# A fused attention and two mixture layers on one core: where an activation copy, tile clears and a split stand in the queues

## The chip, the cores and the metric

The kernel runs on one core of one Trainium2 chip. The metric is the time of one execution in microseconds on the device; lower is better. The core has five engines, each with its own queue: TensorE (PE) multiplies, VectorE (DVE) and ScalarE (ACT) work element by element, GpSimd (POOL) does so too and issues scatters, SyncE (SP) issues DMAs. An engine takes its instructions in the order of its queue. Where two engines depend on each other, one waits on a semaphore.

## The reference, cut to what matters

```python
q_bits = (np.einsum('bhsd,dk->bhsk', q, proj) > 0)
mask = q_bucket[:, :, :, None] == k_bucket[:, :, None, :]
scores = np.where(mask, scale * np.matmul(q, k.transpose(0, 1, 3, 2)), -1000000000.0)
...
h = x @ w_in
sp = np.where(h > 20.0, h, np.log1p(np.exp(np.minimum(h, 20.0))))
x = (h * np.tanh(sp)) @ w_out
...
expert_idx = np.argmax(logits, axis=1)
h = np.maximum(x[mask] @ w1[e], 0.0)
out[mask] = gate_w[mask, None] * (h @ w2[e])
```

Attention has 2 batches, 8 heads, 768 tokens and 64 dimensions; a query sees only keys with the same six hash bits. Its output, 1536 tokens by 512, goes through a dense layer of 2048 hidden units with the activation h·tanh(softplus(h)), and then through one of eight experts of 1024 hidden units.

## The kernel before

**Numbers as pairs.** To keep precision with 16-bit matmuls, most operands are held as two f16 planes, a rounded upper half and the remainder. A product is then three matmuls (upper by upper, upper by lower, lower by upper). ACT usually writes the upper half, and DVE or POOL subtracts to get the lower one.

**Attention** (`Attn`). The constructor makes the constant tiles. There are three tiles `kq` of 128 x 1572 f16 (`NBUF`), used in turn by the heads; line 167 clears each, line 168 sets one column. Lines 172 to 190 clear parts of the tiles `vn` and `sv`. A first head is loaded; `hi` (L265, ACT) makes the upper halves of k and q, `lo` (L271, DVE) the lower halves, one plane at a time, `dup` (L286) copies the upper planes into the head's `kq` tile, next to where `bits` (L307 to L309, DVE) writes the hash planes. `out_x` turns the halves on PE (L229) into PSUM, and the `cx` steps (L231) copy the result out, plane 0 on ACT, plane 1 on DVE. `proj` (L196 to L201, DVE) splits the hash projection in three, and `args` (L297, PE) multiplies with it. The first steps of heads 0 to 4 are written out by hand in `PRO` (line 51), one line a step; a letter at the end (a, d, s, o, m) names the engine of a copy or the PSUM pool. `run_all` (L488) issues them in that order, and `in_order` (L124) makes every engine keep it. From then on a table of due times (`AT`) places the steps of each head in the loop over groups g. The constants ahead of `run_all` are outside `in_order`: the framework's scheduler places them in the queues.

**Other constants** (`Moe.__init__`, L621 to L651) come earlier in the program: biases, iotas, a tile of ones, and `ohacc`, a small count of 128 x 8. Line 646 clears it on POOL, line 647 writes its first row (eight numbers) on DVE.

**The dense layer** (`moe1`, L809). A step G covers one block of 128 hidden units for a chunk of 512 tokens; there are 3 chunks of 16 blocks, 48 steps, and three more to drain. PE's products are `up` (L790, 12 matmuls, into a PSUM tile h) and x2 (L851, 12 matmuls, adding g of step G - 3 to four sums x2). Up to step 21 (`AHEAD`) the up products run three steps ahead, over four PSUM buffers; in steps 22 to 24 there are none; from step 25 each step makes its own, over two buffers. A buffer of h comes free when L878 has read it.

The activation is a polynomial in tanh. In step G, ACT does L871 (tanh of h), L876 and L882 (squares), L885 (a copy that makes the upper half of g for block G - 1), L888 (Exp), and L900 (a square) for block G. DVE does L873 and L878 for block G - 1, whose result L885 and L886 take, and L895 for block G, which needs Exp's result. POOL does L886, the lower half of g. L895 and L873 read two SBUF tiles each. `fill` (L818) puts side work between them: weight pieces (`w2_load`, L1129 on ACT and L1130 on DVE) and `route`. When a chunk's x2 is complete (f == NF1 - 1, so in steps 18, 34 and 50), `route` (L909) copies its rows out (L923 ACT, L924 DVE), squares them (L930 POOL, L931 ACT), makes logits (L948, PE) and scatters rows to experts (L1036, POOL). The last chunk's route runs alone, with PE's transposes at L936. The whole layer is issued inside `in_order`.

**The experts** (`moe2`, L1148). Per expert 96 up and 48 down matmuls, while the next expert's weights are loaded and split.

Of the kernel before, what the change touches and what calls it, by code (L numbers as in the profile page):

```python
# [15 lines left out]
AF = mybir.ActivationFunctionType  # L16
ALU = mybir.AluOpType
# [25 lines left out]
NBUF, NVB, KXB, KMB = 3, 2, 5, 4  # L43
# [11 lines left out]
lo 0 1  # L55
x 0 s
cx 0 0 a
dup 0 d
proj
cx 0 1 d  # L60
hi 1
warm 0
warm 2
# [71 lines left out]
class Attn:  # L135
    def __init__(self, tc, ctx, q, k, v, proj, ident, ones, xx, dt, rest):
        self.tc, self.nc = tc, tc.nc
        nc = self.nc
        self.q, self.k, self.v = q, k, v
        self.ident, self.ones = ident, ones  # L140
        self.xx, self.rest_pools = xx, rest
        self.ld = ctx.enter_context(tc.tile_pool(name="ld", bufs=2))
        self.st = ctx.enter_context(tc.tile_pool(name="st", bufs=2))
        self.pp = ctx.enter_context(tc.tile_pool(name="pp", bufs=2))
        self.sm = ctx.enter_context(tc.tile_pool(name="sm", bufs=2))
        self.ou = ctx.enter_context(tc.tile_pool(name="ou", bufs=1))
        self.dt = dt
        cp = ctx.enter_context(tc.tile_pool(name="acp", bufs=1))
        self.ps_s = ctx.enter_context(tc.tile_pool(name="ps_s", bufs=2, space=PSUM))
        self.ps_m = ctx.enter_context(tc.tile_pool(name="ps_m", bufs=2, space=PSUM))  # L150
        self.ps_o = ctx.enter_context(tc.tile_pool(name="ps_o", bufs=2, space=PSUM))

        self.Z = {}
        warm = cp.tile([P, 1], F32, name="warm")
        nc.vector.memset(warm, 0.0)
        nc.scalar.activation(warm, warm, AF.Exp)
        pj = cp.tile([P, NB], F32, name="pj")

        def load_pj():
            for i in range(2):  # L160
                nc.sync.dma_start(pj[i * D : (i + 1) * D, :], proj)

        self.load_kq(0, 0, load_pj)
        self.KQ, self.VN, self.SV = [], [], []
        for i in range(NBUF):
            kq = cp.tile([P, 2 * KQW], F16, name=f"kq{i}")
            nc.gpsimd.memset(kq, 0.0)
            nc.gpsimd.memset(self.rows(kq, 780)[:, 0, :, 96:97], 1024.0)
            self.KQ.append(kq)


        for i in range(NVB):
            vn = cp.tile([P, NJ, 65 + P], F32, name=f"vn{i}")
            nc.gpsimd.memset(vn[:, :, 64:66], 1.0)
            nc.gpsimd.memset(vn[:, :, 66 : 65 + 64], 0.0)
            self.VN.append(vn)
        self.sel = cp.tile([P, 3], F32, name="sel")
        nc.gpsimd.memset(self.sel, 64.0)
        nc.gpsimd.memset(self.sel[:, 0:1], 0.0)
        self.c98 = cp.tile([P, 1], F32, name="c98")  # L180
        nc.gpsimd.iota(self.c98, pattern=[[0, 1]], base=0, channel_multiplier=1, allow_small_or_imprecise_dtypes=True)
        c97 = cp.tile([P, 1], F32, name="c97")
        nc.vector.tensor_scalar(c97, self.c98, 97.0, 64.0 * S, op0=ALU.is_equal, op1=ALU.mult)
        nc.vector.tensor_scalar(self.c98, self.c98, 98.0, -1.0, op0=ALU.is_equal, op1=ALU.mult)
        for i in range(2):
            sv = cp.tile([P, 3 * P], F16, name=f"sv{i}")
            nc.gpsimd.memset(sv, 0.0)
            for c in (64, P):
                nc.vector.tensor_copy(sv[96:99, c : c + 1], c97[96:99, :])
            self.SV.append(sv)  # L190

        self.pj = cp.tile([P, 3, NB], F16, name="pj3")
        pr = cp.tile([P, NB], F32, name="pjr")
        C = 1.5 * 2.0**17

        def split():  # L196
            nc.vector.tensor_scalar(self.pj[:, 0], pj, C, C, op0=ALU.add, op1=ALU.subtract)
            nc.vector.tensor_tensor(pr, pj, self.pj[:, 0], op=ALU.subtract)
            nc.vector.tensor_copy(self.pj[:, 1], pr)
            nc.vector.tensor_tensor(pr, pr, self.pj[:, 1], op=ALU.subtract)  # L200
            nc.vector.tensor_copy(self.pj[:, 2], pr)  # L201

        self.proj = split
# [397 lines left out]
CAP = 256  # L601
# [15 lines left out]
C1, C2, C3 = 0.48890862, -0.94632237, -0.89895009  # L617


class Moe:  # L620
    def __init__(self, tc, ctx, a, ident, xh, xl):  # L621
        self.tc, self.nc, self.a, self.ident, self.xh, self.xl = tc, tc.nc, a, ident, xh, xl
        nc = self.nc
        cp = self.cp = ctx.enter_context(tc.tile_pool(name="mcp", bufs=1))
        self.dr = ctx.enter_context(tc.tile_pool(name="dr", bufs=1, space=bass.MemoryType.DRAM))
        self.xs = self.dr.tile([E0 * CAP, ROW], U32, name="xs")
        self.xr = self.dr.tile([NT // P, P, ROW], U32, name="xr")

        self.half = cp.tile([P, NR], F32, name="half")
        nc.gpsimd.memset(self.half, 0.5)  # L630
        self.bias = {}
        for v in (0.5, -1.5, C2, C3):
            t = cp.tile([P, 1], F32, name=f"bias{len(self.bias)}")
            nc.gpsimd.memset(t, v)
            self.bias[v] = t
        self.iota = cp.tile([P, NR, E0], F32, name="iota8")
        nc.gpsimd.iota(self.iota, pattern=[[0, NR], [1, E0]], base=0, channel_multiplier=0, allow_small_or_imprecise_dtypes=True)
        self.ones = cp.tile([P, P], F16, name="ones16")
        nc.gpsimd.memset(self.ones, 1.0)
        self.tri = cp.tile([P, P], F16, name="tri")  # L640
        make_upper_triangular(nc, self.tri, val=1.0, diag=False)
        self.tok = cp.tile([P, NT // P], I32, name="tok")
        for b in range(B):
            nc.gpsimd.iota(self.tok[:, b * NJ : (b + 1) * NJ], pattern=[[P, NJ]], base=b * S, channel_multiplier=1)
        self.ohacc = cp.tile([P, E0], F16, name="ohacc")
        nc.gpsimd.memset(self.ohacc, 0.0)
        nc.vector.tensor_scalar(self.ohacc[0:1, :], self.iota[0:1, 0, :], float(CAP), None, op0=ALU.mult)
        self.scat = []
        self.h = {}
        self.later, self.lows, self.soon = [], [], []  # L650
        self.eo = cp.tile([P, NT // P], F32, name="eo")  # L651
# [157 lines left out]
    def moe1(self, side, more):  # L809

        nc, tm = self.nc, self.tm
# [6 lines left out]
        def fill(k=1):  # L818

            nonlocal now  # L820
            for _ in range(k):
                now += 1
                if self.lows:
                    self.lows.pop(0)()
                    continue
                for x in side:
                    if x[0] <= now:
                        x[0] += next(x[1], 1 << 30)
                        side.append(side.pop(side.index(x)))
                        break  # L830

        for G in range(N + GLAG):
            c, F = divmod(G, NF1)
            if G == 0:
                t, w, u, p = m[0] = self.m0
            elif G < N:
                t, w, u, p = m[G] = [T(tag, G) for tag in "twup"]
# [31 lines left out]
            new_step = 0 < G < N  # L869
# [11 lines left out]
            if new_step:  # L881
                nc.scalar.activation(u, w, AF.Square, scale=C1, bias=self.bias[C2])  # L882
            fill(FILL[1])
            if old:
                nc.scalar.copy(g[G - 1][:, 0, :], p1)  # L885
                nc.gpsimd.tensor_tensor(g[G - 1][:, 1, :], p1, g[G - 1][:, 0, :], op=ALU.subtract)  # L886
            if new_step:
                nc.scalar.activation(u, u, AF.Exp, bias=self.bias[C3])  # L888
            while self.later:
                self.later.pop(0)()  # L890
            for x in new[:NC]:
# [507 lines left out]
```

## Time and profile before

| | us |
|---|---|
| median of 3 runs | 732.04 |
| lowest and highest run | 731.93, 736.9 |
| the profiled execution | 732.01 |
| its span in the trace | 729.9 |

The span is the time from the first to the last thing that the trace records on the core; the profiled execution's own time is 2.1 us longer. Times of rows are counted from the span's start. A row of a timeline says start, length, engine, line, operation, output<-inputs, and in brackets how long the engine idled before and who released it. Equal instructions that follow one another are merged into one row, with their count. A DVE record can contain time in which the instruction was held.

### The profile page before, as it was taken

To read this page: it belongs to the slowest core of one execution; us is meant where nothing else is said; L and a number is where in the kernel's file an instruction comes from. 1 tells how busy PE (TensorE), PEld (TensorE's weight loads), DVE (VectorE), ACT (ScalarE), POOL (GpSimd) and SP (SyncE) were. 2 spreads that over 40 slices of the span, in tenths; PEclk is the share of its full clock that TensorE was granted. 3 is DMA by queue.
4 is the path that set the end of the run, shared out by engine and by line. 5 is a ranking of instruction groups with operands and counts; after the bars stand their busy time and mean duration, and the time that the engine had idled before them with its cause. 6 is when DMAs were issued, how large, how long until landed. Compare 5 with 4: busy or idle time off the path is not lost. (4 is left out here: it accounts for less than half of the span.)

```text
span 729.9 us, 10738 instructions
## 1 busy us (share of the span) xinstructions
PE 703.9 (96%) x3997; PEld 383.8 (53%) x3997; DVE 463.2 (63%) x778; ACT 478.4 (66%) x735; POOL 191.0 (26%) x213
## 2 busy tenths in 40 slices
PE   7899999999999999999999899999999999999995
PEld 4454445455455544444444444444448666667772
DVE  7877888787777795565566555545556545565540
ACT  4657576676666597888888866877763455464631
POOL 5211323131312352121224334352422101100111
PEclk9999999999999999999999999999998999999999
DMA  6368688999987243310103001120145879799740
GB/s 174 105 184 216 162 215 226 239 220 274 209 208 171 78 146 106 80 59 0 58 29 74 16 1 59 61 52 4 52 152 180 219 222 275 221 227 269 224 143 20
DMA packets 125644, 102.71 MB, mean 141 GB/s; under 512 B 86391, under 2 KB 104823, under 8 KB 125586
## 3 DMA queue, kind: packets, MB, share of 16 engines
q1 hardware_dynamic: 112514, 81.23, 42.4%
q10 hardware_dynamic: 10832, 14.43, 5.6%
q0 software_dynamic: 2240, 6.31, 2.6%
q8 instruction: 33, 0.54, 0.3%
q14 instruction: 25, 0.20, 0.1%
HBM read 63.52 MB, written 24.26 MB: 120 GB/s over the span
## 5 line engine op out<-in xcount | busy, mean ns | idle before, releaser
L414 PE MATMUL o<-p,vn 128*65 128x384 f32 (+1 forms) x384 | 153.9, 487 | 2.5 <-ACT su L439 2.5
L790 PE MATMUL h<-xx,wi 128*128 128x512 f16 x576 | 133.2, 382 | 3.7 <-DVE p L878 3.6
L851 PE MATMUL x<-wo,g 128*128 128x512 f16 x576 | 131.7, 379 | 1.2 <-POOL g L886 0.6
L375 ACT ACTIVATE p<-s 128x768 f32<-128x768 f32 x96 | 77.2, 807 | 47.4 <-PE s L373 42.2
L895 DVE SCALAR_TENSOR_TENSOR p<-w,u 128x512 f32<-128x512 f32 x47 | 52.0, 1106 | 79.2 <-ACT u L888 79.2
L886 POOL TENSOR_TENSOR g<-p,g 128x512 f16<-128x512 f32 x47 | 54.5, 1159 | 158.8 <-ACT g L885 139.6
L790 PEld LDWEIGHTS <-wi 128*128 128x128 f16 x576 | 56.4, 98 | 72.6 <-issue 7.1
L851 PEld LDWEIGHTS <-g 128*128 128x128 f16 x576 | 56.2, 98 | 70.2 <-POOL g L886 1.1
L1188 PE MATMUL y<-b,hh 128*128 128x512 f16 x384 | 84.2, 379 | 0.0
L1174 PEld LDWEIGHTS <-a 128*128 128x128 f16 x768 | 75.1, 98 | 10.8 <-issue 0.6
L337 DVE TENSOR_REDUCE mx<-ms 128x1 f32<-128x512 f32 x96 | 65.4, 688 | 21.9 <-PE ms L336 21.0
L414 PEld LDWEIGHTS o<-p,vn 128*65 128x65 f32 (+1 forms) x384 | 59.0, 163 | 30.7 <-issue 11.6
L1174 PE MATMUL h<-xt,a 128*128 128x256 f16 x672 | 74.7, 273 | 0.3 <-DVE hh L1181 0.3
L900 ACT ACTIVATE t<-p,bias 128x512 f32<-128x512 f32 x47 | 34.0, 722 | 43.6 <-DVE p L895 43.6
L667 DVE SCALAR_TENSOR_TENSOR b<-st,b 128x1024 f16<-128x1024 f32 x28 | 33.1, 1222 | 45.3 <-ACT b L666 45.3
L1188 PEld LDWEIGHTS <-hh 128*128 128x128 f16 x384 | 37.5, 98 | 43.6
L1193 POOL DMA_INDIRECT out_dram<-o,row x16 | 20.7, 1291 | 147.2 <-ACT o L1192 109.1
L666 ACT ACTIVATE b<-st 128x1024 f16<-128x1024 f32 x28 | 28.0, 1048 | 40.9 <-DMA st<-in_moe_w_dram 37.5
L341 DVE TENSOR_REDUCE mx<-ms 128x2 f32<-128x512 f32 x48 | 33.0, 688 | 28.2 <-PE ms L340 28.2
L873 DVE SCALAR_TENSOR_TENSOR t<-t,u 128x512 f32<-128x512 f32 x48 | 33.6, 700 | 24.6 <-ACT t L900 23.8
L371 PE MATMUL s<-tx 128*128 128x384 f16 x192 | 48.2, 333 | 0.0
L729 POOL TENSOR_TENSOR wi<-cv,wi 128x512 f16<-128x512 f32 x16 | 19.7, 1232 | 106.9 <-ACT cv L728 84.0
(197 smaller groups left out, 1031.5 us busy)
## 6 DMA issues: line engine op xcount, KB each, us to landing
st<-in_moe_w_dram SPq DMA_DIRECT2D x32, 1024.0 KB
stg<-in_moe_w_in_dram SPq DMA_DIRECT2D x16, 512.0 KB
stg<-in_moe_w_out_dram SPq DMA_DIRECT2D x16, 512.0 KB
dx<-ka ACTq DMA_DIRECT2D x12, 384.0 KB
dm<-kq ACTq DMA_DIRECT2D x12, 384.0 KB
xs<-zrow SPq DMA_DIRECT2D x16, 257.0 KB
vn<-in_v_dram SPq DMA_DIRECT2D x16, 192.0 KB
rb<-rd SPq DMA_DIRECT2D x16, 192.0 KB
```

The costliest lines, as they stand in the source:

```text
L337: nc.vector.tensor_reduce(z["mx"][:, j, 0:1], s, axis=AX.X, op=ALU.max)
L371: nc.tensor.matmul(s[:, c, :], kq[:, 0, ts], kq[:, 1, c * HS : (c + 1) * HS], start=True, stop=False)
L375: nc.scalar.activation(p.rearrange("p (c n) -> p c n", c=2), s, AF.Exp, scale=2.0**-11)
L414: nc.tensor.matmul(o, self.vn(b, h, t), z["p"][t][:, cs], start=(t == 0), stop=False)
L790: self.nc.tensor.matmul(h, self.wi[wu][:, k, fs], x[:, k, xs], start=(i == 0), stop=(i == 3 * NKT - 1))
L851: nc.tensor.matmul(x2[r], gf[:, gu, rs], self.wo[wu][:, f, :], start=(f == 0 and gu + wu == 0), stop=(f == NF1 - 1 and gu == 1))
L873: nc.vector.scalar_tensor_tensor(t1, t1, 0.75, u1, op0=ALU.add, op1=ALU.mult)
L886: nc.gpsimd.tensor_tensor(g[G - 1][:, 1, :], p1, g[G - 1][:, 0, :], op=ALU.subtract)
L895: nc.vector.scalar_tensor_tensor(p, w, 1.0, u, op0=ALU.add, op1=ALU.mult)
L900: nc.scalar.activation(t, p, AF.Square, bias=self.bias[-1.5])
L1174: nc.tensor.matmul(h[:, v, :], W[0][wu][:, k, fs], xt[e][:, xu * NKT + k, :], start=(i == 0), stop=(i == 3 * NKT - 1))
L1188: nc.tensor.matmul(y[s], hs[F // 2][:, hu, F % 2, s * P : (s + 1) * P], W[1][wu][:, F, :], start=(F == 0 and hu + wu == 0), stop=(F == NF2 ...
```

## The change

- In `PRO`, the step `dup 0 d` (the copy of head 0's upper planes on DVE, L286) moves from before `proj` and the second `cx` to behind them.
- The clears of `kq` at line 167 are put on DVE for the first two tiles; the third stays on POOL. Line 168 stays on POOL for all.
- The small product at line 647 is put on POOL instead of DVE.
- In `moe1`, Exp (L888) is issued ahead of the copy L885 and of L886. DVE's queue keeps its order, and so does POOL's.

```diff
@@ -55,9 +55,9 @@
 x 0 s
 cx 0 0 a
-dup 0 d
 proj
 cx 0 1 d
+dup 0 d
 hi 1
@@ -164,7 +164,7 @@
             kq = cp.tile([P, 2 * KQW], F16, name=f"kq{i}")
-            nc.gpsimd.memset(kq, 0.0)
+            (nc.gpsimd if i == NBUF - 1 else nc.vector).memset(kq, 0.0)
             nc.gpsimd.memset(self.rows(kq, 780)[:, 0, :, 96:97], 1024.0)
@@ -644,7 +644,7 @@
         nc.gpsimd.memset(self.ohacc, 0.0)
-        nc.vector.tensor_scalar(self.ohacc[0:1, :], self.iota[0:1, 0, :], float(CAP), None, op0=ALU.mult)
+        nc.gpsimd.tensor_scalar(self.ohacc[0:1, :], self.iota[0:1, 0, :], float(CAP), None, op0=ALU.mult)
@@ -881,11 +881,11 @@
             fill(FILL[1])
+            if new_step:
+                nc.scalar.activation(u, u, AF.Exp, bias=self.bias[C3])
             if old:
                 nc.scalar.copy(g[G - 1][:, 0, :], p1)
                 nc.gpsimd.tensor_tensor(g[G - 1][:, 1, :], p1, g[G - 1][:, 0, :], op=ALU.subtract)
-            if new_step:
-                nc.scalar.activation(u, u, AF.Exp, bias=self.bias[C3])
             while self.later:
```

## Rows read from the trace of the kernel before

**Rows 1.** The page, busy time: us (share of the span) xinstructions.
```profile
PE 703.9 (96%) x3997; PEld 383.8 (53%) x3997; DVE 463.2 (63%) x778; ACT 478.4 (66%) x735; POOL 191.0 (26%) x213
```

**Rows 2.** What PE waited for: us in total, times, longest us.
```profile
PE h L790 <- DVE p L878: 3.6, 2, 3.2
...
PE psx L229 <- DVE ka L271: 0.8, 1, 0.8
...
PE x L851 <- POOL g L886: 0.6, 1, 0.6
```

**Rows 3.** Timeline of PE about the longest wait.
```profile
411.64 2.75 PE L851 MATMUL x<-wo,g 128*128 128x512 f16 x12
414.23 1.35 PE L948 MATMUL lg<-enT,xt 128*128 128x8 f16 x48
418.82 4.44 PE L790 MATMUL h<-xx,wi 128*128 128x512 f16 x12 [3.24 <-DVE p L878]
```

**Rows 4.** One microsecond behind it: busy times, PEclk, DMA share, GB/s.
```profile
421.00:422.00 1.00, 1.00 (x4) 0.44 (x3) 0.66 (x1) 0.30 (x1) 1.00 (x2) 0.50 0.00 0
```

**Rows 5.** Timeline of ACT, one step of the dense layer.
```profile
302.03 0.72 ACT L900 ACTIVATE t<-p,bias 128x512 f32<-128x512 f32 x1 [1.19 <-DVE p L895]
...
303.27 0.72 ACT L876 ACTIVATE w<-t,bias 128x512 f32<-128x512 f32 x1
304.02 0.72 ACT L882 ACTIVATE u<-w,bias 128x512 f32<-128x512 f32 x1
304.65 0.60 ACT L885 CAST g<-p 128x512 f16<-128x512 f32 x1
305.16 0.72 ACT L888 ACTIVATE u<-u,bias 128x512 f32<-128x512 f32 x1
...
307.07 0.72 ACT L900 ACTIVATE t<-p,bias 128x512 f32<-128x512 f32 x1 [0.68 <-DVE p L895]
```

**Rows 6.** Timeline of DVE, the same step.
```profile
305.98 1.06 DVE L895 SCALAR_TENSOR_TENSOR p<-w,u 128x512 f32<-128x512 f32 x1 [1.78 <-ACT u L888]
```

**Rows 7.** Timeline of POOL, the same step.
```profile
305.33 1.16 POOL L886 TENSOR_TENSOR g<-p,g 128x512 f16<-128x512 f32 x1 [3.88 <-ACT g L885]
```

**Rows 8.** Groups by line, DVE from 284 to 288 us: busy us, mean ns.
```profile
L805 DVE SCALAR_TENSOR_TENSOR w<-w,u 128x512 f32<-128x512 f32 x1 | 0.7, 693 | 4.0 <-ACT u L803 4.0
```

**Rows 9.** Timeline of ACT, in steps 19 and 21.
```profile
382.98 0.62 ACT L885 CAST g<-p 128x512 f16<-128x512 f32 x1 [0.50 <-DVE p L878]
...
395.10 0.61 ACT L931 ACTIVATE sq<-sq 128x512 f32<-128x512 f32 x1
```

**Rows 10.** Timeline of PE, the second chunk's end and the layer's end.
```profile
465.49 2.75 PE L851 MATMUL x<-wo,g 128*128 128x512 f16 x12 [0.26 <-DVE row L924]
468.61 2.75 PE L790 MATMUL h<-xx,wi 128*128 128x512 f16 x12 [0.36 <-DVE p L878]
...
529.73 7.93 PE L851 MATMUL x<-wo,g 128*128 128x512 f16 x36
...
541.37 1.50 PE L936 MATMUL tp<-ident,row 128*128 128x128 f16 x24
```

**Rows 11.** Timeline of DVE, the prologue.
```profile
2.43 4.41 DVE L647 TENSOR_SCALAR ohacc<-iota 1x8 f16<-1x8 f32 x1 [1.55 <-POOL ohacc L646]
4.69 2.15 DVE L271 SCALAR_TENSOR_TENSOR ka<-kq,ka 128x384 f16<-128x384 f32 x2
...
9.87 1.02 DVE L271 SCALAR_TENSOR_TENSOR ka<-kq,ka 128x384 f16<-128x384 f32 x2
10.80 0.35 DVE L286 COPY kq<-ka 128x768 f16<-128x768 f16 x1
```

**Rows 12.** Timeline of POOL, the prologue.
```profile
2.33 4.09 POOL L167 MEMSET kq<- 128x1572 f16 x3
```

**Rows 13.** Timeline of PE, the prologue.
```profile
2.09 4.02 PE L210 MATMUL warmed<-ones 128*128 128x384 f16 x12 [2.09 <-POOL ones L639]
...
6.92 0.84 PE L229 MATMUL psx<-ident,ka 128*128 128x128 f16 x12 [0.82 <-DVE ka L271]
```

## The prediction, written before the kernel was changed

> **What bounds the kernel now.** The page first: TensorE (PE) is busy for 703.9 of 729.9 us [rows 1]. So the end moves only by what PE loses, and the list of what PE waited for comes next [rows 2]. For this change three of its entries count: 3.6 us, in two waits, for VectorE's (DVE) product at L878, which frees a buffer of h; 0.8 us in the prologue for the lower halves of L271; 0.6 us for the activations' lower half from GpSimd (POOL), L886. The chain that ended last shows only the output's scatter.
>
> Then PE's timeline at the longest wait [rows 3]. PE is through with the logits at 414.23 + 1.35 = 415.58, but the next up product starts at 418.82, held for 3.24 us by L878. That product then takes 4.44 us where the x2 product of equally many matmuls took 2.75: the granted clock is 0.50 behind the wait [rows 4], the lower of the two levels, after an engine that stood idle. The one place costs 3.24 + 1.69 = 4.93 us.
>
> Why is L878 late? One step of the dense layer with little side work, on ScalarE (ACT), [rows 5] shows a recurrence: L900 of a step starts at 302.03, L900 of the next at 307.07, a period of 5.04 us. In it ACT copies the activations (L885, 304.65) and only then runs Exp (L888, 305.16). Exp feeds L895 on DVE, which starts at 305.98 and takes 1.06 us [rows 6], and L900 waits for L895. L885 also releases POOL's L886 at 305.33 for 1.16 us [rows 7], so POOL runs just ahead of L895 and across it. The same operation with POOL idle, L805, took 693 ns [rows 8]. PE's two products per step start 414.23 - 411.64 = 2.59 us apart [rows 3], some 5.2 us a step: the recurrence has nothing to spare, and any side work puts it behind PE.
>
> **Exp ahead of the copy.** No instruction is added or removed, 47 steps are reordered. The new period from rows 5, 6 and 8: L900 to L876 1.24, L876 to L882 0.75, L882 to Exp 0.75 (Exp now depends on the instruction just ahead of it, as L882 does on L876), Exp to L895 0.82, L895 0.69, L895's end to L900 0.03. Sum 4.28 us, 0.76 below 5.04: the copy's slot goes (0.51 saved, less 0.12 for the dependence) and L895 is shorter by 0.37, since L886 can start only behind the copy, as L895 ends. Bounds for L895's saving: 0 if POOL still meets it, 0.37 if never; I take 0.37, since Exp to copy's end is 0.63 + 0.60 and Exp to L895's end 0.82 + 0.69, so POOL can overlap a tail at most.
>
> Does that cure the wait? By the code the first chunk's x2 is complete in step 18, where the row copies tie ACT to PE, and the held product (step 27) needs L878 of step 26, some seven steps later. Needed: 3.24 us. Available: 7 x 0.76 = 5.3. Against it, side work shared a gap with nothing before and now shares it with the copy: between Exp and L900, 0.82 + 0.69 + 0.03 - 0.63 = 0.91, less 0.51 for the copy, leaves 0.40. A square like that of L931 (0.61) [rows 9] or a weight copy of the same size overflows by 0.1 to 0.4 with its read-out, about 2.3 us over six steps. For it: in step 19 the copy waited 0.50 us for L878 with Exp behind it [rows 9]; Exp no longer stands there. 5.3 - 2.3 + 0.5 = 3.5 us, which is enough, though barely, and a lead gathered in steps 1 to 17 lets the row copies start at the first finished quarter rather than the last. I take the wait and its slow clock as gone: 4.9 us. What is late next is PE itself: up products then follow at PE's own rate.
>
> Two further places in the dense layer. At the second chunk's end the up products start at 465.49 + 3.12 = 468.61, 0.5 us over 2.59, and x2 at 465.49 was itself held by L924 for 0.26 [rows 10]; with the chain earlier by the copy's slot I take 0.8 for both (bounds 0 and 0.8). At the end, 36 matmuls start at 529.73, so the last dozen could run from 529.73 + 3 x 2.59 = 537.50 to 540.09; the transposes behind it started at 541.37, 1.28 later [rows 10], because copy and L886 of the last step were late. That step has no Exp of its own, but its input comes a slot and a contention earlier, over 1 us: I take 1.2 (0.3 to 1.6). Copies come later by 0.63 within a step; what hides that is the lag of three steps between g and its x2, about 15 us, and four buffers of g. If that cover were gone each step would cost 0.6.
>
> The new order turns the port question round: L886 now runs where L873, which also reads two SBUF tiles, comes up after L900. The Trainium skill (SBUF — State Buffer, Who interferes with whom) says that a DVE instruction with two SBUF inputs and a GpSimd instruction that reads SBUF exclude each other, the first holding on to its end. Rows 6 and 7 agree: L895 ended 0.55 us behind L886. By that rule L873 waits up to 0.3 us per step; it is off the recurrence, so the sum stays, and the rule taken to its extreme is the rival below that ends slower.
>
> **Clears, the small product and the split, in the prologue.** DVE starts L647 at 2.43 and is held for 4.41 us for eight elements, to 6.84; POOL's three clears of kq fill 2.33 to 6.42 [rows 11, 12]. Behind L647 stand L271 and the split (L286), and PE's first transposes start at 6.92, having waited 0.82 [rows 13]. After: POOL does L647 itself and one clear of three; two clears, 2.7 us, leave it. DVE does them from about 0.9 on, with nothing to wait for. Their price on DVE is in no row: from below, the f16 copy of 768 elements at 0.35, so 0.7 each; from above, L271 (384 elements, half of 1.02 for two), so 2.1 each [rows 11]; nearest is POOL's own clear of the same tile at 1.4 [rows 12]. I take 1.4: ready at 3.7, before the first L271 starts at 4.69, so hidden by the wait for the input. At 2.1 each they end at 5.1 and delay L271 by 0.4. The Trainium skill (VectorE: DVE Perf Modes, Zero memsets can be issued as uint32) prices a clear at one cycle per element; with that page's clock an estimate is 1.64 us each, ready at 4.2, and by it the sum would be the same.
>
> L271's two then run 4.69 to 5.7. PE's warm-up product ends at 2.09 + 4.02 = 6.11 [rows 13], which is late next: the transposes gain 6.92 - 6.11 = 0.8 us; with the dear clears DVE is done at 6.1 and the gain is the same less 0.1. L647 on POOL: at least nothing, at most a whole clear's 1.4; POOL still is 1.3 us earlier, and nobody on the path waits for it. Moving L286 behind the second copy adds 0.35 us [rows 11] where DVE waits for the projection's matmuls on PE, and takes it from ahead of the split of proj; cover gone, it costs 0.35. No DMA is issued by any moved step. I take 0.8; bounds -0.7 (an initialising DVE instruction queued ahead of L271 waits for POOL) and 1.3 (a filler of DVE drops out of the path too). DVE and PE carry this shift into the attention loop, whose waits are between engines, not on DMA.
>
> Sum: 4.9 + 0.8 + 1.2 + 0.8 = 7.7, plus some 0.5 of short delays like those above that the list of waits leaves out, 8.2 us. The profiled execution took 732.01 us (span 729.9), the median of the runs is 732.04, so both give 723.8.
>
> **Rivals.** (1) Half a cure: POOL still meets L895, a step gains 0.39. 7 x 0.39 - 2.3 + 0.5 = 0.9, so 2.3 us of the wait stay, and the slow clock with it: 0.9 + 0.8 + 0.6 + 0.4 = 2.7, 729.3. For it: POOL has other work (squares). Against: the order of Exp and copy decides, POOL can't pass the copy. (2) The swap gives nothing, since ACT is the limit and not the recurrence: 0.8 from the prologue, 731.2. Against: ACT stood idle 1.19 us ahead of L900 where a step had no side work [rows 5]. (3) Slower: L873 is held by L886 and, if POOL keeps the port from one instruction to the next, by its square too; L878 comes later, and DVE reaches the next L895 late. It decides from about 1.5 us of holding per step, where the 0.76 is eaten (L873's slack to the next L895 is some 0.8). In seven steps 0.5 each lengthens the wait by 3 us: 732.0 + 3 - 0.8 = 734. Against: L895 took the port as soon as L886 ended. (4) Better: the route behind the dense layer escapes part of its slow clock by the shift: 722.
>
> **Chances.** Forecast 0.67 (own range 722.5 to 726), (1) 0.15, (2) 0.07, (3) 0.05, (4) 0.06. The range, 721 to 729.3, leaves out most of (2) and (3). A measurement of this kernel tells about 1% (7.3 us, 724.7) from no change: faster 0.6 (two thirds or more of the forecast's own case, and the fourth), same 0.35, slower 0.05.
>
> **What would show it.** Right: L895 near 0.7 us; period 4.3 in steps where h is ready; no PE wait for L878 near 407 to 415 and no clock of 0.50 there; first transposes near 6.1; L647 a fraction of a microsecond on POOL. Wrong: L895 still above 1 us, L873 above 1.5 us, the wait at the 27th up product still over 2 us, or clears on DVE that end behind 5 us.

## The result, and the profile after

The changed kernel takes 724.64 us (median of 4 runs, 721.95 to 725.62), the kernel before 733.52 in the same session (4 runs, 731.93 to 736.9). The ratio is 0.9867, 95% interval 0.9827 to 0.9907. The forecast was 723.8, with 721 to 729.3 as its range. The profiled execution took 725.26 us, its span is 723.2; before it was 732.01 and 729.9, so the two traces compared below stand 6.7 us apart, somewhat less than the medians.

The page's busy times, the answer to [rows 1]: PE has lost 4.6 us of busy time for the same matmuls, so part of the gain is products that run faster, and its share rose by a point.

```profile
PE 699.3 (97%) x3997; PEld 382.3 (53%) x3997; DVE 457.2 (63%) x779; ACT 482.8 (67%) x735; POOL 188.5 (26%) x212
```

What PE waited for, as in [rows 2]: the waits for L878, for L271 and for POOL's lower half at L851 have left the list. Third now stands one in the experts, L1174 for L1181, which has grown by 1.8 us.

```profile
PE o L414 <- ACT su L439: 2.5, 3, 0.9
PE warmed L210 <- POOL ones L639: 2.1, 1, 2.1
PE h L1174 <- DVE hh L1181: 2.1, 2, 1.7
```

The same entry before the change:

```profile
PE h L1174 <- DVE hh L1181: 0.3, 1, 0.3
```

PE's timeline at the place of [rows 3], and at the layer's end [rows 10]. The up product of step 27 follows the logits with no bracket, in 2.75 us instead of 4.44. At the end 48 matmuls run in one row and the transposes start 532.44 - 522.08 = 10.36 us behind its first, which is 4 x 2.59: nothing is lost there.

```profile
410.00 2.75 PE L851 MATMUL x<-wo,g 128*128 128x512 f16 x12
412.59 1.35 PE L948 MATMUL lg<-enT,xt 128*128 128x8 f16 x48
413.80 2.75 PE L790 MATMUL h<-xx,wi 128*128 128x512 f16 x12
...
522.08 10.52 PE L851 MATMUL x<-wo,g 128*128 128x512 f16 x48
532.44 1.50 PE L936 MATMUL tp<-ident,row 128*128 128x128 f16 x24
```

The microsecond of [rows 4] again: the clock is 1.00, the upper level.

```profile
421.00:422.00 1.00, 1.00 (x7) 0.47 (x5) 0.94 (x2) 0.00 (x0) 0.26 (x1) 1.00 0.00 0
```

One step on ACT (Exp is now L885, the copy L887), as in [rows 5]: Exp directly behind the square, the copy in the gap while L895 runs, 381.32 - 377.03 = 4.29 us from one L900 to the next, where it was 5.04.

```profile
377.03 0.71 ACT L900 ACTIVATE t<-p,bias 128x512 f32<-128x512 f32 x1
...
379.01 0.72 ACT L882 ACTIVATE u<-w,bias 128x512 f32<-128x512 f32 x1
379.77 0.72 ACT L885 ACTIVATE u<-u,bias 128x512 f32<-128x512 f32 x1
380.39 0.60 ACT L887 CAST g<-p 128x512 f16<-128x512 f32 x1
381.32 0.72 ACT L900 ACTIVATE t<-p,bias 128x512 f32<-128x512 f32 x1 [0.32 <-DVE p L895]
```

DVE and POOL about the same step and the next (POOL's lower half is now L888). L895 takes 0.69 us, against 1.06 in [rows 6], and POOL starts as it ends. The price is paid by L873, L1130 and POOL: at 387.07 L873 takes 1.64 us, held by POOL's square L930, which had itself waited for DVE's L1130, as the order of their ends shows.

```profile
380.59 0.69 DVE L895 SCALAR_TENSOR_TENSOR p<-w,u 128x512 f32<-128x512 f32 x1 [0.81 <-ACT u L885]
382.07 0.77 DVE L873 SCALAR_TENSOR_TENSOR t<-t,u 128x512 f32<-128x512 f32 x1 [0.79 <-ACT t L900]
...
385.86 1.28 DVE L1130 SCALAR_TENSOR_TENSOR b<-st,b 128x512 f16<-128x512 f32 x1 [0.28 <-ACT b L1129]
387.07 1.64 DVE L873 SCALAR_TENSOR_TENSOR t<-t,u 128x512 f32<-128x512 f32 x1
```

POOL's timeline, the same stretch:

```profile
381.07 1.22 POOL L888 TENSOR_TENSOR g<-p,g 128x512 f16<-128x512 f32 x1 [12.82 <-ACT g L887]
...
385.37 1.22 POOL L888 TENSOR_TENSOR g<-p,g 128x512 f16<-128x512 f32 x1 [1.51 <-ACT g L887]
386.56 1.60 POOL L930 TENSOR_TENSOR sq<-row 128x512 f32<-128x512 f16 x1
```

The prologue, to be laid beside [rows 11 to 13]: on DVE the two clears end at 2.56, and nothing holds the first L271 but its input; on POOL one clear is left, and L647 takes 0.53 us; on PE the first transposes start at 5.45, with no wait, behind the warm-up product. DVE's timeline:

```profile
1.02 1.54 DVE L167 MEMSET kq<- 128x786 uint32 x2
4.77 1.03 DVE L271 SCALAR_TENSOR_TENSOR ka<-kq,ka 128x384 f16<-128x384 f32 x2 [2.21 <-ACT ka L265]
...
7.80 0.35 DVE L286 COPY kq<-ka 128x768 f16<-128x768 f16 x1
```

The timeline of POOL there:

```profile
2.33 1.41 POOL L167 MEMSET kq<- 128x1572 f16 x1
...
4.91 0.53 POOL L647 TENSOR_SCALAR ohacc<-iota 1x8 f16<-1x8 f32 x1
```

The timeline of PE there:

```profile
2.09 3.52 PE L210 MATMUL warmed<-ones 128*128 128x384 f16 x12 [2.09 <-POOL ones L639]
5.45 0.92 PE L229 MATMUL psx<-ident,ka 128*128 128x128 f16 x12
```

**Where the time went, by marks on PE.** The marks are the first x2 of the dense layer (L851), the transposes behind its last (L936), and the span's end.

| | first x2 | dense layer: first x2 to transposes | transposes to the end | span |
|---|---|---|---|---|
| before | 297.23 | 244.14 | 188.53 | 729.9 |
| after | 296.04 | 236.40 | 190.76 | 723.2 |

So 1.19 us come from ahead of the dense layer and 7.74 from it, and 2.23 went again in route and experts, 1.8 of which is the longer wait at L1174. Whether that loss belongs to the change is a question for the experiments.

### The profile page after: what moved, and what is told of

It is laid out like the page before. It is cut to its first block, busy times and chain, and to the rows that moved or that the text cites. A ratio compares the mean times of both kernels' runs of the same rounds, so it can differ in the third digit from the quotient of the medians.

```text
span 723.2 us, 10738 instructions
## 1 busy us (share of the span) xinstructions
PE 699.3 (97%) x3997; PEld 382.3 (53%) x3997; DVE 457.2 (63%) x779; ACT 482.8 (67%) x735; POOL 188.5 (26%) x212
## 5 line engine op out<-in xcount | busy, mean ns | idle before, releaser
L790 PE MATMUL h<-xx,wi 128*128 128x512 f16 x576 | 131.5, 379 | 0.0
L851 PE MATMUL x<-wo,g 128*128 128x512 f16 x576 | 131.3, 379 | 0.0
L888 POOL TENSOR_TENSOR g<-p,g 128x512 f16<-128x512 f32 x47 | 56.5, 1202 | 152.5 <-ACT g L887 133.8
L851 PEld LDWEIGHTS <-g 128*128 128x128 f16 x576 | 56.4, 98 | 68.0 <-POOL g L888 0.3
L1174 PEld LDWEIGHTS <-a 128*128 128x128 f16 x768 | 75.0, 98 | 12.8 <-issue 2.6
L337 DVE TENSOR_REDUCE mx<-ms 128x1 f32<-128x512 f32 x96 | 65.4, 688 | 21.8 <-PE ms L336 20.8
L1174 PE MATMUL h<-xt,a 128*128 128x256 f16 x672 | 74.8, 273 | 2.1 <-DVE hh L1181 2.1
L895 DVE SCALAR_TENSOR_TENSOR p<-w,u 128x512 f32<-128x512 f32 x47 | 32.5, 692 | 63.2 <-ACT u L885 58.8
L873 DVE SCALAR_TENSOR_TENSOR t<-t,u 128x512 f32<-128x512 f32 x48 | 38.6, 805 | 23.1 <-ACT t L900 22.3
L373 PE MATMUL s<-tm 97*128 97x384 f16 x192 | 47.0, 325 | 0.0
```

The costliest lines, as they stand in the source:

```text
L337: nc.vector.tensor_reduce(z["mx"][:, j, 0:1], s, axis=AX.X, op=ALU.max)
L373: nc.tensor.matmul(s[:, c, :], m[0:97, 0, ts], m[0:97, 1, c * HS : (c + 1) * HS], start=False, stop=True)
L790: self.nc.tensor.matmul(h, self.wi[wu][:, k, fs], x[:, k, xs], start=(i == 0), stop=(i == 3 * NKT - 1))
L851: nc.tensor.matmul(x2[r], gf[:, gu, rs], self.wo[wu][:, f, :], start=(f == 0 and gu + wu == 0), stop=(f == NF1 - 1 and gu == 1))
L873: nc.vector.scalar_tensor_tensor(t1, t1, 0.75, u1, op0=ALU.add, op1=ALU.mult)
L1174: nc.tensor.matmul(h[:, v, :], W[0][wu][:, k, fs], xt[e][:, xu * NKT + k, :], start=(i == 0), stop=(i == 3 * NKT - 1))
```

## The experiments

**The swap alone, and all but the swap.** First the kernel before with Exp ahead of the copy and nothing else.

```diff
+            if new_step:
+                nc.scalar.activation(u, u, AF.Exp, bias=self.bias[C3])
             if old:
                 nc.scalar.copy(g[G - 1][:, 0, :], p1)
...
-            if new_step:
-                nc.scalar.activation(u, u, AF.Exp, bias=self.bias[C3])
```

> Kernel before with Exp ahead of the copy, nothing else. If the dense layer's part is independent of the prologue: first transposes at 6.9 us as before, dense layer (first x2 product to the last route's transposes) near 236.4 us as in the changed kernel instead of 244.1, no wait of PE for L878 behind the logits, L895 near 0.69 us. Time 732 - 7.7 = about 724.5 to 726. Rival (the prologue's shift is needed for it, since it changes where the phases fall): the wait at the up product of step 27 is partly there and the time is above 728.

Measured: 723.75 us (median of 4, 722.83 to 725.83), ratio 0.9853 (0.982 to 0.9887) against 733.13 for before (13 runs). The dense layer took 236.39 us, L895 692 ns in the mean, and the up product of step 27 came without a wait. Then the reverse, the changed kernel with the old order of copy and Exp.

```diff
             if old:
                 nc.scalar.copy(g[G - 1][:, 0, :], p1)
                 nc.gpsimd.tensor_tensor(g[G - 1][:, 1, :], p1, g[G - 1][:, 0, :], op=ALU.subtract)
+            if new_step:
+                nc.scalar.activation(u, u, AF.Exp, bias=self.bias[C3])
```

> Changed kernel with the old order of copy and Exp: only clears, small product and split are moved. Theory: first transposes at 5.4 to 6.1 us, first maximum (L337) at 11.2 to 12.5 instead of 13.6, the dense layer starts 1.2 us earlier and takes the 244 us of before with the wait of about 3.2 us for L878 back. Time 730.5 to 731.3. Rival (the prologue's gain is swallowed in the attention loop): 732, dense layer starting at 297.2.

Measured: 732.35 us (10 runs), ratio 0.999 (0.9968 to 1.0013). The first x2 comes 1.21 us earlier than before, as the theory had it, but the time is the rival's: the dense layer takes 245.28, with the wait back. PE's timeline of this kernel:

```profile
412.74 1.35 PE L948 MATMUL lg<-enT,xt 128*128 128x8 f16 x48
417.63 5.28 PE L790 MATMUL h<-xx,wi 128*128 128x512 f16 x12 [3.54 <-DVE p L878]
```

What follows: the swap makes the whole gain of the dense layer, and all of the gain that a measurement can tell. The layer took 236.39 or 236.40 us in each of the eight profiles here with the swap alone or under other edits of the prologue, and 243.79 to 245.37 in the four that keep the old order and POOL's lower half. The three prologue edits win about a microsecond at the first x2, here and in the first profile of the changed kernel, and none that ten runs can show.

**The changed kernel once more**, to see what spreads by itself; no edit.

> The changed kernel once more, for the spread: the expert phase (from the first expert's up product to the end) took 175.0 us before and 177.1 after in one execution each. If that difference belongs to the change (weights come later relative to PE), it is about 177 here too and PE waits some 2 us for L1181. If it is the spread of the weight loads, it lies between 175 and 178 with other waits. All before that phase should repeat within 0.3 us. Time 722 to 726.

Measured: 723.91 us (4 runs, 721.65 to 727.18), ratio 0.9849 (0.9812 to 0.9887). In this profile the dense layer takes 236.39 again, and PE's waits for L1181 are 0.4 us in all. But the first x2 comes at 300.52, 4.5 us later than in the first profile of the same program, where a repeat within 0.3 was expected. All of it is lost by 95 us: the mean granted clock is 0.94 in the stretches 0 to 30 and 60 to 90 us, 1.00 in the first profile, and PE waits 1.61 us for L307 at 81 us. A third time, in another session:

> The changed kernel a third time, beside the version with both edits of the prologue and the kernel before: 722 to 726 us, dense layer 236.4 us, first x2 between 295.7 and 300.5 us.

Measured: 725.06 us (8 runs, 723.22 to 731.04), ratio 0.9898 (0.9866 to 0.993), dense layer 236.39, first x2 at 295.62. Over the three sessions the median of 16 runs is 724.7 us. In the fourteen profiles of this study the stretch from the transposes to the end took 188.1 to 192.5 us in the nine whose dense layer was cured, and 188.5 to 190.6 in the five others. The wait at L1174 is 0.2 to 3.2 us where it appears. So the 2.23 us lost behind the layer lie within what one program shows from run to run; they are not the change's.

**Only the small product on POOL** (the kernel before, with L647 alone moved).

```diff
-        nc.vector.tensor_scalar(self.ohacc[0:1, :], ...
+        nc.gpsimd.tensor_scalar(self.ohacc[0:1, :], ...
```

> Kernel before with only the small product (L647) on POOL; all three clears of kq stay on POOL, the split stays ahead. Theory (DVE's queue stood behind L647, which POOL's clears held off; L271 itself is not held by clears, which only write): L271 starts near 4.7 and each takes 0.55, first transposes at 5.5 to 6.1 us; the split (L286, a two-port copy) is then the one that is held until a clear ends, near 6.4. Rival (the clears hold every DVE instruction): L271 ends near 6.8 and the transposes start at 6.9 as before.

Measured: 735.98 us (one run). The timeline of DVE in this kernel:

```profile
4.73 1.03 DVE L271 SCALAR_TENSOR_TENSOR ka<-kq,ka 128x384 f16<-128x384 f32 x2 [3.85 <-ACT ka L265]
5.67 1.37 DVE L286 COPY kq<-ka 128x768 f16<-128x768 f16 x1
...
8.40 0.34 DVE L183 TENSOR_SCALAR c<-c 128x1 f32<-128x1 f32 x1
```

and PE's:

```profile
5.66 0.83 PE L229 MATMUL psx<-ident,ka 128*128 128x128 f16 x12
...
8.80 0.47 PE L297 MATMUL ar<-pj,tx 128*128 128x18 f16 x12 [1.98 <-DVE c L183]
```

L271, two SBUF inputs, runs unheld while POOL clears, and the transposes start 1.26 us earlier. But the copy L286 is held to 7.04, past the end of the three clears at 6.42, and a constant of DVE (L183), which the scheduler now puts ahead of the copy that PE needs, waits for a POOL iota behind those clears: PE waits 1.98 us and the hash planes come at 10.06, 0.3 later than before. The edit alone gains nothing.

**Only the clears on DVE** (the kernel before, with line 167 changed).

```diff
-            nc.gpsimd.memset(kq, 0.0)
+            (nc.gpsimd if i == NBUF - 1 else nc.vector).memset(kq, 0.0)
```

> Kernel before with only the two clears on DVE; the small product stays on DVE, the split stays ahead. Theory: L647 is held by POOL's single clear to about 3.8 us, which ends ahead of the first L271 at 4.7: transposes at 5.5 to 6.1 us, as with all three edits. Rival (the small product has to go): L271 later than 5.2 us.

Measured: 732.57 us (one run). L647 is still on DVE and still held, to 4.55 where 3.8 was expected (two small clears of POOL, L175, follow the one of `kq` and end at 4.54), but it ends in time (timeline of DVE in this kernel):

```profile
2.47 2.08 DVE L647 TENSOR_SCALAR ohacc<-iota 1x8 f16<-1x8 f32 x1
4.64 1.03 DVE L271 SCALAR_TENSOR_TENSOR ka<-kq,ka 128x384 f16<-128x384 f32 x2
```

The first hash maximum (L337) starts at 11.04, against 13.60 before and 11.17 after the whole change: the clears alone give the gain at this mark. At the first x2, 297.24, nothing of it is left in this profile. **The split put back ahead of proj** in the changed kernel is the third part:

```diff
 cx 0 0 a
+dup 0 d
 proj
 cx 0 1 d
-dup 0 d
```

> Changed kernel with the split put back ahead of proj and the second copy. Theory: the split takes 0.35 to 0.8 us at 5.7, all of DVE behind it slips by 0.35 to 0.5, so L309 ends 0.3 to 0.5 us later than the 9.0 of the changed kernel; the dense layer starts up to 0.4 us later. Rival (the wait for the projection hides it): L309 at the same time within 0.1.

Measured: 723.75 us (one run). L309 and the first maximum come 0.23 us later (9.05, 11.40) than in the first profile of the changed kernel; in its other two the maximum is at 11.11 and 11.27. Nothing of it is left at the first x2 (295.74). What follows: of the three edits one carries the first maximum, one is worth 0.1 to 0.3 us there, and one only does no harm once the clears are gone.

**Only the contention taken away** (the kernel before, its order kept, the lower half on DVE).

```diff
-                nc.gpsimd.tensor_tensor(g[G - 1][:, 1, :], p1, ...
+                nc.vector.tensor_tensor(g[G - 1][:, 1, :], p1, ...
```

> Kernel before, order of copy and Exp kept, but the lower half of g (L886) is made on DVE instead of POOL: the port question is taken away and the copy's slot stays. Theory (both parts count, 0.39 for the slot and 0.37 for the port): L895 near 0.69 us, period of a quiet step near 4.65 to 4.7, and the wait of PE for L878 behind the logits about 3.2 - 7 x 0.37 = 0.7 us or less. Rival (only the order counts): period stays near 5.04 and the wait near 3.2 us. DVE has 0.7 us more to do per step, which can bring a wait of its own at the chunks' ends.

Measured: 725.7 us (one run), L895 692 ns, and a step of 4.61 us, even with a weight copy in it, which fits the gap behind Exp (timeline of ACT in this kernel):

```profile
356.93 0.72 ACT L900 ACTIVATE t<-p,bias 128x512 f32<-128x512 f32 x1 [0.76 <-DVE p L895]
...
360.69 0.61 ACT L1129 ACTIVATE b<-st 128x512 f16<-128x512 f32 x1
361.54 0.72 ACT L900 ACTIVATE t<-p,bias 128x512 f32<-128x512 f32 x1 [0.24 <-DVE p L895]
```

and PE's timeline at the place of the long wait:

```profile
413.44 1.35 PE L948 MATMUL lg<-enT,xt 128*128 128x8 f16 x48
414.65 2.75 PE L790 MATMUL h<-xx,wi 128*128 128x512 f16 x12
```

The long wait is gone here too, and the dense layer takes 236.89 us, 0.5 more than with the swap. Half of the cure is enough.

**The copy twice** (the changed kernel, L887 issued a second time as L888, to put the price of one copy back without the contention).

```diff
                 nc.scalar.copy(g[G - 1][:, 0, :], p1)
+                nc.scalar.copy(g[G - 1][:, 0, :], p1)
```

> The changed kernel with the copy of the upper half (L887) issued twice in every step of the dense layer that has one: one more ACT instruction of about 0.61 us per step, behind Exp, with the same result. Theory (the recurrence from one L900 to the next sets the pace, and the copy now fills the gap that ACT has while L895 runs): of the gap of about 0.9 us the first copy takes 0.5, so the second overflows by some 0.1 to 0.3 beyond what is left in a quiet step, the period goes from 4.3 to about 4.8 to 4.9, still under PE's 5.2; in steps with side work ACT falls behind by up to 0.6 each. The slack of 1.95 us before the up product of step 27 loses about 7 x 0.5 = 3.5, so a wait for L878 comes back there of some 1.5 us, with the slow clock behind it: dense layer 237.5 to 240 us. Rival (what ACT gathers as a lead in steps 1 to 17, and the time that its row copies wait for PE, covers it, as taking only the contention away did): no wait, dense layer 236.4 to 236.9 us. L895 stays at 0.69 us in both.

Measured: 731.12 us (one run, beside 733.68 of before). A step with nothing else (L901 at 378.04 to L901 at 382.59) takes 4.55 us, less than the 4.8 to 4.9 expected and less than in the experiment above, but a step with a weight copy or a square has no gap left to put it in; the one shown, from ACT's timeline in this kernel, takes 5.14 us:

```profile
409.51 0.71 ACT L901 ACTIVATE t<-p,bias 128x512 f32<-128x512 f32 x1
...
412.87 0.60 ACT L887 CAST g<-p 128x512 f16<-128x512 f32 x1
413.50 0.62 ACT L888 CAST g<-p 128x512 f16<-128x512 f32 x1
414.03 0.62 ACT L932 ACTIVATE sq<-sq 128x512 f32<-128x512 f32 x1
...
414.65 0.71 ACT L901 ACTIVATE t<-p,bias 128x512 f32<-128x512 f32 x1
```

PE's timeline of this kernel, with the wait:

```profile
413.47 1.35 PE L949 MATMUL lg<-enT,xt 128*128 128x8 f16 x48
416.86 2.75 PE L790 MATMUL h<-xx,wi 128*128 128x512 f16 x12 [2.03 <-DVE p L878]
```

The wait returned with 2.03 us where some 1.5 were expected, and the dense layer took 241.76 us, above the 237.5 to 240 of the theory; the rival (a lead that covers all) fell. The layer lost more than the one wait: PE also waited 0.95 for a tile of the route behind it (L996), and 0.25 and 0.68 for g at its end. The slow clock that was expected behind the wait did not come: the product took 2.75.

The four kernels side by side settle how the wait is decided. All times in this table count from the start of PE's x2 row of 36 matmuls (before at 395.96, after at 394.46, lower half on DVE at 395.31, copy twice at 395.34). The first column is L900 behind the first chunk's row copies, the second the same instruction seven steps on, the third the end of the L878 that frees the buffer. PE wants that buffer at 413.80 - 394.46 = 19.34. (The waits in PE's rows, 3.24 and 2.03, are 0.1 to 0.2 shorter than the last column has them.)

| | L900 behind the row copies | L900 seven steps on | L878 ends | against 19.34 |
|---|---|---|---|---|
| before | -16.21 | 20.64 | 22.81 | 3.47 late |
| after | -17.43 | 15.06 | 17.39 | 1.95 early |
| lower half on DVE | -17.43 | 15.69 | 17.86 | 1.48 early |
| copy twice | -17.30 | 19.31 | 21.47 | 2.13 late |

A seventh of the way from the first column to the second is a step: 5.26 us before, 4.64 after, 4.73 and 5.23 in the experiments. What counts over these seven steps is the step with side work, not the quiet one.

The rows behind the first line of the table, from the timelines of ACT and DVE before:

```profile
379.75 0.73 ACT L900 ACTIVATE t<-p,bias 128x512 f32<-128x512 f32 x1
...
416.60 0.72 ACT L900 ACTIVATE t<-p,bias 128x512 f32<-128x512 f32 x1 [0.63 <-DVE p L895]
418.08 0.69 DVE L878 SCALAR_TENSOR_TENSOR p<-t,h 128x512 f32<-128x512 f32 x1
```

and behind the second, after (its first row, L900 at 377.03, is shown above), with one of the copies that came late:

```profile
399.40 0.62 ACT L887 CAST g<-p 128x512 f16<-128x512 f32 x1 [0.34 <-DVE p L878]
...
409.52 0.71 ACT L900 ACTIVATE t<-p,bias 128x512 f32<-128x512 f32 x1
411.16 0.69 DVE L878 SCALAR_TENSOR_TENSOR p<-t,h 128x512 f32<-128x512 f32 x1
```

**What bounds the prologue now.** Two experiments on the changed kernel. In the first the six small constant instructions of lines 183 to 189 go behind the copies of the second product:

```diff
 cm 0 1 d
+consts
...
+        def consts():
```

> Changed kernel with six small constant instructions of DVE (L183, L184, L189) moved behind the copies of the m planes. In the changed kernel they stand between the parts of the split of proj, and PE waits 0.8 us for its last part (L201). Theory: L201 ends near 6.8 instead of 7.4 and the first maximum comes 0.5 us earlier, but the next stage waits for the load of heads 2 and 3 (ACT waited 0.33 us for it), so at most 0.2 us reach the dense layer. Rival: DVE's order in the prologue is the bound up to the loop, and 0.5 us reach the end.

Measured: 724.85 us (4 runs), ratio 0.9869 (0.983 to 0.9907). Proj's split ended about half a microsecond earlier, yet the first maximum came at 11.20, directly behind the moved constants, which now fill DVE's queue ahead of it from 10.48 on. And ACT waited 1.32 us for the load of heads 2 and 3, which then is late. So that load was brought forward:

```diff
+        self.load_kq(0, 2)
         self.load_v(0, 0)
-        self.load_kq(0, 2)
```

> The changed kernel with the load of heads 2 and 3 of q and k issued ahead of the load of v at the head of the loop that drives attention. Theory (since the clears left DVE's way, the second pair's load is the next thing late in the prologue): the first L265 of heads 2 and 3, which waited 0.3 to 1.3 us for this load in the changed kernels, starts up to 0.3 us earlier and waits no more; the first hash maximum and L362 move by 0 to 0.3 us; the load of v arrives later, but its first reader is late. Rival (the load's place in the queue does not set its arrival, since all issues are early and the transfers share the DMA engines): the second pair comes at the same time or v's tiles come late and something waits for them. Both: the dense layer stays at 236.4 us and the time within 2 us of the changed kernel's.

Measured: 722.64 us (one run). ACT's L265 of heads 2 and 3 started at 10.49 instead of 10.83, with no wait, and L362 at 18.68 instead of 19.02, as the theory had it; the first maximum did not gain (11.27 against 11.17). The dense layer took 236.39. Then both edits together:

> The changed kernel with both edits on the next bounds of the prologue: the load of heads 2 and 3 ahead of the load of v, and the three small constants of DVE behind the copies of the second product. Theory (with the constants gone from between the parts of proj and the load there in time, the first maximum is bound by PE and the chain of head 0): proj's split ends 0.4 to 0.5 us earlier, ACT's L265 of heads 2 and 3 does not wait for its load, and the first hash maximum comes 0.1 to 0.4 us earlier, at 10.8 to 11.1 us; the attention loop starts 0.3 to 0.7 us earlier (L362 at 18.3 to 18.7); the time is 0 to 1.5 us under that of the changed kernel, which five rounds may not tell. Rival (the attention loop's own waits take it back): L362 earlier, but the first x2 at 296 us as in the changed kernel, and no difference in time.

Measured: 722.98 us (5 runs, 722.52 to 725.25), ratio 0.9852 (0.9826 to 0.9879), beside 0.9898 for the changed kernel in the same session. The first maximum is at 10.95, L362 at 18.48, the first x2 at 294.35, each the earliest of all kernels here. The two intervals overlap: this version may be better than the changed kernel by a microsecond or two, but that is not shown.

## Why the prediction was right, and where its terms were off

**The cause** was right: the copy on the recurrence and the contention behind it delayed L878, and PE stood idle and then ran slow. The quiet step was forecast at 4.28 us and measured 4.29; L895 at 0.69, measured 0.692; the wait and the clock of 0.50 are gone. That the swap and nothing else does this is shown by the pair of kernels with and without it.

**The dense layer's terms** (4.9 for the wait with its slow clock, 0.8, 1.2, and 0.5 unlisted: 7.4) measured 7.74. From the start of the 36-matmul row to the end of step 27's up product the traces give 27.30 before and 22.09 after, 5.2 for the first term; the layer's end gives 1.28, all that was lost there. At the second chunk's end 0.95 us were lost before and 0.18 are lost now (462.48 to 468.61 against 455.59 to 460.95 for two products of 2.59), so 0.77 for the 0.8; 0.48 is left for the unlisted ones.

**The margin** was the weakest step: 5.3 - 2.3 + 0.5 = 3.5 us against 3.24, "enough, though barely". By the table the buffer came 3.47 + 1.95 = 5.42 us earlier. Seven steps gave 36.85 - 32.49 = 4.36 of it. The toll for side work in the new order came out near its size: 32.49 - 7 x 4.29 = 2.46, put at 2.3 (0.70 of it is L873's, see below). Too small was the credit for what the old order lost in the same steps, 36.85 - 7 x 5.04 = 1.57, put at 0.5. The lead with which ACT met the row copies gave another 1.22; the prediction named it and put no number to it. L873, held by POOL, took 0.16 back. The two missing credits made rival (1) too dark: it left 2.3 us of the wait for a half cure. Its own mixture, slot gone and contention kept, was not tried, but the opposite half, contention gone and slot kept, has a like quiet step (0.43 saved, to rival 1's 0.39) and ends the wait with 1.48 us to spare.

**L873** was foreseen to wait up to 0.3 us. Its mean in the dense layer rose from 701 to 811 ns, but four took 1.64 to 1.70, three of them in the seven steps of the table: POOL does L888 and a square one behind the other, and DVE's L1130 took a turn between them. So one of the prediction's own signs of being wrong, L873 above 1.5 us, did show, and L873 was not wholly off the recurrence: twice in the seven steps L878 came late behind it and the copy started 0.36 and 0.34 us late (389.54 and 399.40; for the first of these waits the profile names PE, but L878 had ended 0.11 us before), 0.70 of the 2.46. This is rival (3)'s mechanism, present in a few steps and far from the 1.5 us per step from which it would decide. The Trainium skill (SBUF — State Buffer, Who interferes with whom) has it that a DVE instruction with two SBUF inputs and a GpSimd instruction that reads SBUF exclude each other, whoever is first holding on. The rows agree from both sides: L895 took 1106 ns in the mean with L886 across it and 692 without, L873 701 before and 811 with L888 near it.

**The prologue's clears** were taken at 1.4 us each (0.7 to 2.1) and measured 0.77: the trace shows 786 words of 32 bits where the tile has 1572 halves. The result was to be the same, and was. The Trainium skill (VectorE: DVE Perf Modes, Zero memsets can be issued as uint32) has it that a clear costs by its elements and that the wider type halves them; the prediction counted the halves, and by the words that page's clock gives an estimate of 0.82 us, near the measured 0.77.

**The prologue's gain** was put at 0.8 us with PE's warm-up next. That bound held, with the transposes at 5.45 in the first profile and 5.6 to 5.9 in the others instead of 6.1. Missed was what follows: the second product's transposes took 1.44 us before and take 0.83 now, so the first maximum is 2.43 us earlier. PE's timeline before:

```profile
10.10 1.44 PE L229 MATMUL psm<-ident,kq 128*128 128x128 f16 x12 [1.24 <-DVE kq L309]
```

and after:

```profile
9.16 0.83 PE L229 MATMUL psm<-ident,kq 128*128 128x128 f16 x12 [0.91 <-DVE kq L309]
```

The granted clock is 0.52, 0.50 and 0.50 in the microseconds from 10 to 13 before, and 1.00 throughout after. (With the swap alone that row reads 1.00 too, although the same transposes take 1.44 there: the durations agree from profile to profile, the row does not.) Attention gave half of the gain back: 1.78 is left at L362, 1.19 at the first x2. There the three profiles of the changed kernel scatter from 295.62 to 300.52, which is more than the gain. The lower bound, -0.7 for a DVE constant that waits behind POOL's clears, is close to what the small product alone ran into, with the constant ahead of a copy instead of L271.

**The total.** 8.2 us were forecast from profile to profile, 6.75 came: dense layer and prologue gave 8.9, the experts' spread took 2.2. The medians, 733.5 and 724.6, are 8.9 apart. That 723.8 and 724.64 lie so close is in part luck: the forecast took 8.2 from 732.0, while the medians give 8.9 from 733.5. Rival (2) is excluded by the swap alone. Rival (4)'s route did not move in the first two traces (13.57 us before, 13.62 after, from the transposes to the first expert's product); in the other profiles it takes 10.6 to 13.8 with the swap and 12.3 to 13.6 without.

## What to carry to other kernels

Where an engine's step is a recurrence through another engine, issue first what the other waits for, and put independent work into the gap that opens; then count the steps that carry side work, since they and not the quiet ones decide whether the gap holds. The order on one engine also decides which of two others meet at a shared port: a copy moved by one place took a contention of 0.4 us off the critical instruction and laid it on one with more slack, which was enough in five of the seven steps that counted. And of several edits to a prologue, ask what the first big loop does with the lead: here it kept about half in a trace, nothing in another, and no timing could tell it.

## What the runs showed of the hardware, unexpected

- A wait of PE does not always bring the slow clock. Behind 3.24 and 3.54 us the up product took 4.44 and 5.28 us; behind the 2.03 us of the kernel with two copies it took 2.75, and the clock stayed at 1.00.
- POOL's clears held DVE's one-input instructions (eight elements of L647 for 4.41 us, the f16 copy L286 for 1.37 instead of 0.35), while the two-input L271 ran at its usual 1.03 for two during the same clears. L647 ended 0.01 us behind a small clear of POOL (L175) in the kernel before, at 6.84, and with the clears on DVE, at 4.55: it got no turn between clears that followed one another.
- DVE and POOL took turns: L888 on POOL ended at 386.59, L1130 on DVE at 387.14, L930 on POOL at 388.16, L873 on DVE at 388.71. Each ended 0.55 us (DVE) or 1.02 us (POOL) behind the one before it, though its record is 1.28 to 1.64 us long, most of it holding.
